# A fifth tile of at most 64 tokens computed in 16 products instead of 24, in a retention and mixture-of-experts kernel

## The chip, the cores and the metric

The kernel runs on one core of a Trainium2 chip. The metric is the device time of one execution in microseconds, the median of several runs. The core has TensorE (PE; PEld is its weight load), VectorE (DVE), ScalarE (ACT), GpSimd (POOL), and SyncE (SP), which issues DMAs; POOL issues the indirect ones (gathers and scatters by row numbers). The engines run beside each other, each through its own instructions in program order, and wait for each other by semaphores.

## What is computed

```python
attn = ((scale * q @ k.T) * Dmat) @ v           # 8 batches, 8 heads, 576 positions, 64 wide; Dmat: causal decay
x = attn.transpose(0, 2, 1, 3).reshape(4608, 512)
logits = normed(x) @ normed(expert_emb).T / tau   # 8 experts
expert_idx = argmax(logits, 1); gate_w = softmax(logits)[expert_idx]
for e in range(8):
    mask = expert_idx == e
    out[mask] = gate_w[mask, None] * (relu(x[mask] @ w1[e]) @ w2[e])   # 512 -> 1024 -> 512
```

All data are float32.

## The kernel before

**Stages.** The first 170 us compute the attention and the routing. Then the experts follow one after another, each in two stages. In the first (mm1, from expert 1 on a list of 28 block products of six matmuls each, in the order `ORDER`) PE computes the hidden layer; in the second (mm2) it multiplies the hidden layer by `w2`. Every float32 operand is kept as a high part and a low part, and a product is the sum of three matmuls: high by high, high by low, low by high.

**Tiles.** An expert has 640 slots for tokens (`CAP`), five tiles of 128. `mm2(e, i)` does tile i: 8 blocks of the hidden layer times three forms, 24 matmuls of 128x512 (L1303) into one PSUM bank, with `hs` (the hidden layer's high and low parts) as weights. ACT then scales the bank by the tokens' gates into `ys[i]` (L1315), and `put_rows` (L1277) scatters its rows to `out` by the row numbers in `sid`; slots without a token have a number out of bounds and are dropped. Gates are gathered by the row numbers in `gid` (L376).

**Counts known only at run time.** `count_left` writes for each expert how many tokens it has beyond 512; PE reads the counts into registers (`rest`). In mm1 each product takes 320 columns if there are over 96 such tokens, 304 if over 64, else 288 (L1234, L1237). In mm2 of experts 1 to 6 the fifth tile is skipped if there are none (L1300).

**Order.** The order on each engine is the order of the code. Two plans put the preparation for the next expert between PE's matmuls: `mm2_plan(e)` has an entry for every third of a tile (0 to 14), `mm1_plan(e)` one for each product (1 to 28). In the fifth tile, which stands under a condition, the tasks come behind all its matmuls. The tasks that matter here: `xturn(n, i)`, a 16-bit copy on ACT (L404) and a transposing DMA on SP's queue (L405), which turns the gathered tokens of the next expert; `xjoin`, `xsums`, `xhigh`, `xlow`, which make the operands of mm1 from them (ACT L411 and L446, DVE L422 to L429 and L450); `w1sum`, `w1hi`, `w1lo`, `w2hi`, `w2lo`, the same for weights (L1145, L1119, L1122; `w1sum(e, 3)` is on POOL).

**Buffers.** `ys` has five tiles. In mm1 they are reused: `follow` (L1249) copies a PSUM bank of block 2 into `ys[4]` behind the 17th product, (6, 2), and the 20th product, (7, 2), adds to the same bank, so that PE may start it only when that copy is done. `w0s` has 8192 columns, of which the weights of mm1 take two times 3584 from expert 1 on.

Of the kernel before, what the change touches and what calls it, by code (L numbers as in the profile page):

```python
# [24 lines left out]
DM = H * D  # L25
NE = 8
FF = 1024
NF = FF // P
NT = N // P
CT = 5  # L30
CAP = CT * P
# [7 lines left out]
HB = P // 2  # L39
HC = CAP // 2  # L40
NPR = NF // 2
# [54 lines left out]
def retention_moe(ctx: ExitStack, tc: tile.TileContext, qk, kn, v0s, vs, w1, w2, head, cst, out):  # L96
# [260 lines left out]

    BEG = group_tiles(B - 3)[0] * P

    def gather(e, i, rows=N):  # L360
        a = e * CT + i
        t = xg[e, i] = raws[(2, 3, 6)[i]] if (e, rows) == (0, BEG) else raws[(i + 1) % 7]
        nc.gpsimd.indirect_dma_start(  # L363
            out=t[:, XO : XO + DM],
            out_offset=None,
            in_=xd[:rows, :],
            in_offset=bass.IndirectOffsetOnAxis(ap=gid[:, a : a + 1], axis=0),
        )

    def gather_gates(e, a0=0, a1=CT):  # L370
        if a0 == 0:
            gts[e] = mg.tile([P, CT], F32, name="gt")
        g = gts[e]
        for i in range(a0, a1):
            a = e * CT + i
            nc.gpsimd.indirect_dma_start(  # L376
                out=g[:, i : i + 1],
                out_offset=None,
                in_=gd[:, :],
                in_offset=bass.IndirectOffsetOnAxis(ap=gid[:, a : a + 1], axis=0),  # L380
            )

    def xsplit(i, u):
# [98 lines left out]
        nc.vector.tensor_copy(sid2, f)  # L482

    left = keep.tile([P, NE], I32, name="left")
    rest = []

    def count_left():

        ps = psm.tile([P, 512], F32, name="m")
        nc.tensor.matmul(ps[:, :NE], ones, run, start=True, stop=True)  # L490
        nc.vector.tensor_scalar(
            out=left, in0=ps[:, :NE], scalar1=-float(CAP - P), scalar2=0.0, op0=ALU.add, op1=ALU.max
        )
        done(ps)

# [582 lines left out]
    with ExitStack() as moe:  # L1078
        mw = moe.enter_context(tc.tile_pool(name="mw", bufs=1))
        hs = mw.tile([P, 2, NF, CAP], F32R, name="hs")  # L1080
        xsb = late["xsb"] = mw.tile([P, 10 * CAP], F32R, name="xsb")
        late["xs1"] = xsb[:, : 2 * NP * C1].rearrange("p (s r n) -> p s r n", s=2, r=NP)
        wsa = mw.tile([P, 28 * P], F32R, name="wsa")
# [189 lines left out]

        puts = []

        def put_rows(rows_of_y, k, rows):
            put = nc.gpsimd.indirect_dma_start(  # L1277
                out=out.rearrange("t (k n) -> (t k) n", k=k),
                out_offset=bass.IndirectOffsetOnAxis(ap=rows, axis=0),
                in_=rows_of_y,  # L1280
                in_offset=None,
                bounds_check=N * k - 1,
                oob_is_err=False,
            )
            for other in puts:
                tc.declare_no_dep(put.ins, other.ins, reason="a scatter writes other rows or other columns")
            puts.append(put)

        last_rows = []

        def mm2(e, i, tasks):
            w = w2s.rearrange("p s (f n) -> p s f n", f=NF)
            a = e * CT + i
            y = ys[i]

            step = DM // 2 if a == NA - 1 else DM
            for n in range(0, DM, step):
                ps = psm.tile([P, 512], F32, name="m")
                last = i == CT - 1 and 0 < e < NE - 1
                with tc.If(rest[e] > 0) if last else nullcontext():  # L1300
                    for j, f in enumerate(SECOND):
                        for k, (hsp, ws) in enumerate(((0, 0), (0, 1), (1, 0))):
                            nc.tensor.matmul(  # L1303
                                ps[:, :step],
                                hs[:, hsp, f, i * P : (i + 1) * P],
                                w[:, ws, f, n : n + step],
                                start=(j == 0 and k == 0),
                                stop=(j == NF - 1 and k == 2),
                            )
                            if not last and step == DM and (3 * j + k) % 8 == 7 and 3 * j + k < 23:  # L1310
                                tasks((3 * j + k) // 8)
                if last:
                    tasks(0)
                    tasks(1)
                nc.scalar.activation(y[:, n : n + step], ps[:, :step], AF.Copy, scale=gts[e][:, i : i + 1])  # L1315
                done(ps)
                k = DM // step
                rows = sid[:, a : a + 1] if k == 1 else sid2[:, n // step : n // step + 1]
                part = (y[:, n : n + step], k, rows)
                if a < NA - 2:  # L1320
                    put_rows(*part)
                else:
                    last_rows.append(part)
            tasks(2)
# [5 lines left out]
        def mm2_plan(e):  # L1330
# [64 lines left out]
        for f, ps in zip(PAIRS, first):  # L1395
# [13 lines left out]
            14: [(count_left,), (xturn, 1, 3)],  # L1409
        }  # L1410
        for g in range(NPR, 2 * NF):
            f, q = PAIRS[g % NF], g // NF
# [3 lines left out]
        for e in range(NE):  # L1416
            if e:
                plan = mm1_plan(e)
                for k, (n, i) in enumerate(ORDER, 1):
                    product(e, n, i)  # L1420
                    follow(n, i)
                    if k < len(ORDER):
                        run_tasks(plan, k)
                highs.pop()()
                w2hi(e, 3)
                lows.pop()()
                w2lo(e, 3)
                held.pop()()
                run_tasks(plan, len(ORDER))
# [203 lines left out]
```

## Time and profile before

| | |
|---|---|
| Median of 3 runs | 554.09 us (553.58 to 556.0) |
| Profiled execution | 554.6 us, of which 552.8 us is the span from the first to the last instruction |
| PE busy | 544.5 us, 98% of the span |
| DVE, ACT, POOL busy | 417.2, 375.8, 240.2 us |
| Granted TensorE clock | 1.00 over the whole span |

An mm1 stage lasts 22.6 to 25.1 us, an mm2 stage of five tiles 27.2 us.
A row of a timeline merges like instructions of one engine that follow each other without a gap: its time runs from the first start to the last end, and "xN" is their number. Matmuls overlap, so that the time from one to the next is not the duration of one. What stands in brackets is the engine's idle time before the row and who ended it.

### The profile page before, as it was taken

The page shows a single profiled execution, that of the slowest core. Times are in us where ns is not written, and L with a number is a line of the kernel's source. Part 1 is how long each engine was busy: PE and PEld are TensorE (multiplying, and loading weights), DVE is VectorE, ACT ScalarE, POOL GpSimd, SP SyncE. Part 2 cuts the span into 40 slices and gives each one's busy share as a digit, 9 for nine tenths or more (in the row PEclk, how much of TensorE's full clock was granted, in tenths as well). Part 3 has the DMA queues.
Part 4 walks back from the last instruction along what each step waited for, and adds up shares of the span by engine and source line. Part 5 has one row for each costly group of instructions (what it writes and reads, how often), then busy time and mean ns, then how long its engine had stood idle before and what let it go on. Part 6 is the DMA issues. An engine that isn't in the chain of part 4 may idle for free. (4 is left out here: it accounts for less than half of the span.)

```text
span 552.8 us, 13528 instructions
## 1 busy us (share of the span) xinstructions
PE 544.5 (98%) x5067; PEld 491.3 (89%) x5067; DVE 417.2 (75%) x939; ACT 375.8 (68%) x700; POOL 240.2 (43%) x233
## 2 busy tenths in 40 slices
PE   8999999999999999999999999999999999999996
PEld 8898988898898899889988988998898899889986
DVE  4856778789875967986896789589978948976810
ACT  1256454457767959967895898589879858957511
POOL 6674435543463661265056207603730750343022
PEclk9999999999999999999999999999999999999999
DMA  9999999968459555847765765557567558641211
GB/s 316 390 392 377 376 319 357 377 254 287 149 195 195 169 184 135 170 145 171 156 179 169 148 154 172 171 158 156 177 172 154 171 173 149 159 133 54 77 39 50
DMA packets 81109, 109.57 MB, mean 198 GB/s; under 512 B 42327, under 2 KB 43771, under 8 KB 81024
## 3 DMA queue, kind: packets, MB, share of 16 engines
q1 hardware_dynamic: 71920, 86.24, 54.1%
q0 software_dynamic: 7696, 19.95, 10.8%
q10 hardware_dynamic: 1408, 2.17, 1.2%
q8 instruction: 62, 1.02, 0.8%
q14 instruction: 23, 0.19, 0.1%
HBM read 80.27 MB, written 19.94 MB: 181 GB/s over the span
## 5 line engine op out<-in xcount | busy, mean ns | idle before, releaser
L1303 PE MATMUL m<-w2s,hs 128*128 128x512 f32 x600 | 138.1, 389 | 0.0
L1303 PEld LDWEIGHTS m<-w2s,hs 128*128 128x128 f32 x600 | 112.4, 188 | 23.2
L1277 POOL DMA_INDIRECT out<-y,sid x41 | 50.3, 1227 | 178.9 <-DVE raw L422 122.7
L1303 PE MATMUL a<-w2s,hs 128*128 128x512 f32 (+1 forms) x360 | 78.8, 375 | 0.0
L1303 PEld LDWEIGHTS a<-w2s,hs 128*128 128x128 f32 x360 | 64.2, 188 | 11.9
L363 POOL DMA_INDIRECT raw<-xd,gid x40 | 44.0, 1101 | 29.4 <-ACT xsb L446 11.8
L376 POOL DMA_INDIRECT gt<-gd,gid x40 | 43.9, 1098 | 19.1 <-issue 12.0
L1187 DVE SCALAR_TENSOR_TENSOR hs<-y,hs 128x320 fp32r<-128x320 f32 x84 | 43.8, 528 | 7.6 <-ACT hs L1194 5.6
L411 ACT COPY raw<-raw 128x1024 uint16<-128x1024 uint16 x35 | 47.9, 1367 | 0.8 <-DMA raw<-raw 0.8
L1194 ACT ACTIVATE hs<-y 128x320 fp32r<-128x320 f32 x84 | 39.4, 476 | 12.6 <-DVE y L1245 11.8
L705 POOL TENSOR_TENSOR kt<-kt,cs 128x512 f32<-128x512 f32 x28 | 28.3, 1042 | 44.9 <-DMA kt<-kn 44.9
L1245 DVE TENSOR_TENSOR y<-a,y 128x320 f32<-128x320 f32 x53 | 25.4, 485 | 29.6 <-ACT y L1249 29.2
L1122 DVE TENSOR_TENSOR w2s<-raw,w2s 128x1024 fp32r<-128x1024 f32 x32 | 39.1, 1221 | 8.4 <-ACT w2s L1119 8.3
L1225 PE MATMUL m<-xsb,w0s 128*128 128x288 f32 (+2 forms) x270 | 43.6, 300 | 0.2
L1225 PE MATMUL a<-xsb,w0s 128*128 128x288 f32 (+2 forms) x270 | 43.2, 300 | 0.0
L1315 ACT ACTIVATE y<-m,gt 128x512 f32<-128x512 f32 x26 | 18.0, 691 | 34.3 <-PE m L1303 34.3
L1225 PEld LDWEIGHTS m<-xsb,w0s 128*128 128x128 f32 x270 | 38.8, 188 | 0.6 <-ACT y L1249 0.6
L1225 PEld LDWEIGHTS a<-xsb,w0s 128*128 128x128 f32 x270 | 38.9, 188 | 0.1
L404 ACT COPY raw<-raw 128x1024 uint16<-128x1024 uint16 x35 | 36.7, 1048 | 0.0
L1119 ACT CAST w2s<-raw 128x1024 fp32r<-128x1024 f32 x32 | 33.4, 1043 | 2.9 <-DMA raw<-w 2.9
L724 POOL TENSOR_TENSOR qkt<-qkt,gsb 128x384 f32<-128x384 f32 x32 | 31.3, 1005 | 5.6 <-issue 3.4
L450 DVE TENSOR_TENSOR xsb<-raw,xsb 128x128 fp32r<-128x128 f32 x70 | 30.5, 483 | 0.0
(259 smaller groups left out, 1177.9 us busy)
## 6 DMA issues: line engine op xcount, KB each, us to landing
raw<-w SPq DMA_DIRECT2D x64, 512.0 KB, 4.0
qkt<-qk SPq DMA_DIRECT2D x28, 576.0 KB, 7.4
xd<-y SPq DMA_DIRECT2D x36, 256.0 KB, 9.4
vt<-vs SPq DMA_DIRECT2D x7, 1152.0 KB, 13.0
kt<-kn SPq DMA_DIRECT2D x7, 1024.0 KB, 10.5
qkt<-qk ACTq DMA_DIRECT2D x4, 288.0 KB, 5.5
qkt<-qk SPq DMA_DIRECT2D x4, 288.0 KB, 5.5
out<-y,sid POOLq DMA_INDIRECT x41, 3.4
```

The source lines that it names most:

```text
L363: nc.gpsimd.indirect_dma_start(out=t[:, XO : XO + DM], out_offset=None, in_=xd[:rows, :], in_offset=bass.IndirectOffsetOnAxis(ap=gid[:, a ...
L376: nc.gpsimd.indirect_dma_start(out=g[:, i : i + 1], out_offset=None, in_=gd[:, :], in_offset=bass.IndirectOffsetOnAxis(ap=gid[:, a : a + 1 ...
L404: nc.scalar.copy(far.rearrange("p (h n) -> p h n", h=2), near.rearrange("p (n h) -> p h n", h=2))
L411: nc.scalar.copy(far.bitcast(U16).rearrange("p (n h) -> p h n", h=2), near.rearrange("p (h n) -> p h n", h=2))
L724: nc.gpsimd.tensor_tensor(out=q, in0=q, in1=gsb[:, p, :], op=ALU.mult)
L1119: nc.scalar.copy(hi, u)
L1122: nc.vector.tensor_tensor(out=lo, in0=u, in1=hi.bitcast(F32), op=ALU.subtract)
L1187: nc.vector.scalar_tensor_tensor(out=lo, in0=part(src), scalar=0.0, in1=hi.bitcast(F32), op0=ALU.max, op1=ALU.subtract)
L1194: nc.scalar.activation(hi, part(src), AF.Relu)
L1225: nc.tensor.matmul(ps[:, :n_cols], w[:, ws, ka, d * P : (d + 1) * P], xop(kx, xsp)[:, d, :n_cols], start=(n in (1, 2, 5) and d == 0 and k ...
L1277: put = nc.gpsimd.indirect_dma_start(out=out.rearrange("t (k n) -> (t k) n", k=k), out_offset=bass.IndirectOffsetOnAxis(ap=rows, axis=0), ...
L1303: nc.tensor.matmul(ps[:, :step], hs[:, hsp, f, i * P : (i + 1) * P], w[:, ws, f, n : n + step], start=(j == 0 and k == 0), stop=(j == NF - ...
```

## The change

1. The fifth tile of experts 1 to 6 (`fitted`) gets a third form. With over 64 tokens in it, it runs the 24 matmuls as before; with none it is skipped; with 1 to 64 it runs 16. For this `both_parts` puts, with four copies on DVE (entry 9 of `mm2_plan`), the first 32 of each 64 columns of the high part and of the low part side by side in two free pieces of `w0s` (`ht`). 128 weight columns then hold 64 tokens twice, and the 16 matmuls are `ht` by high `w2` and `ht` by low `w2`. The copies are made for all six experts, whatever their counts.
2. The low rows of such a tile come out in other partitions of `ys[4]` than the high rows. `low_rows` makes row numbers for the gates (`gidx`) and for the low rows (`sidx`): 11 operations on DVE behind `count_left`, which gets one more itself. The first scatter writes the high rows; `add_low` adds the low rows to `out` with a second, adding scatter from `ys[4]`, issued by POOL behind the 10th product of the next mm1, once the first has landed. It is issued for all six experts; where the tile has no low rows, all its row numbers are out of bounds.
3. `xturn(n + 1, 0)`, the copy on ACT and its transposing DMA, moves from entry 8 of the mm1 stage to entry 12 of the mm2 stage ahead of it, between the fifth tile's matmuls and its scaling on ACT.

```diff
+    def fitted(e, i):
+        return i == CT - 1 and 0 < e < NE - 1
...
+            ids = gidx[:, e : e + 1] if fitted(e, i) else gid[:, a : a + 1]
...
+    def low_rows():
+        q = P // 4
+        g, r = tab[:, 0, :NE], tab[:, 1, :NE]
+        nc.vector.memset(r, BIG)
+        nc.vector.tensor_copy(g, fifth(gid))
+        for k in (0, 2):
+            to, of = slice((k + 1) * q, (k + 2) * q), slice(k * q, (k + 1) * q)
+            nc.vector.tensor_copy(g[to], fifth(gid)[of])
+            nc.vector.tensor_copy(r[to], fifth(sid)[of])
...
+        nc.vector.tensor_scalar(
+            out=few, in0=ps[:, :NE], scalar1=float(CAP - P + HB), scalar2=None, op0=ALU.is_le
+        )
...
+        ht = [w0s[:, o : o + NPR * P].rearrange("p (f c) -> p f c", f=NPR) for o in (28 * P, 4096 + 28 * P)]
...
+                compute_op=ALU.add if first else ALU.bypass,
...
+        def both_parts():
+            for k in range(2):
+                for o, v in enumerate(ht):
+                    t = hs[:, k, NPR * o : NPR * (o + 1), (CT - 1) * P :].rearrange("p f (h c) -> p f h c", h=2)
+                    v = v.rearrange("p f (h s c) -> p f h s c", h=2, s=2)
+                    nc.vector.tensor_copy(v[:, :, :, k, :], t[:, :, :, : HB // 2])
+        def add_low(e):
+            put_rows(ys[CT - 1], 1, sidx[:, e : e + 1], firsts[e])
...
+                if fitted(e, i):
+                    with tc.If(rest[e] > HB) as many:
+                        passes(three)
+                    with many.Else():
+                        with tc.If(rest[e] > 0):
+                            passes(((ht, 0), (ht, 1)))
...
+            if fitted(e, CT - 1):
+                plan[9].insert(1, (both_parts,))
...
+            if n + 1 < NE:
+                plan[12].append((xturn, n + 1, 0))
...
-                plan[8] = [(xturn, n, 0)]
...
+                    if k == 10 and fitted(e - 1, CT - 1):
+                        add_low(e - 1)
```

**Fifth tile of expert 2, on PE**, before; `m_71` and `m_69` are the banks of tiles 2 and 3, `m_68` that of the fifth:

```order
L1303 MATMUL m_69<-w2s,hs 128x512 x24
L1300 COMPARE_AND_BRANCH
L1303 MATMUL m_68<-w2s,hs 128x512 x24
L1300 UNCONDITIONAL_BRANCH
L1300 UNCONDITIONAL_BRANCH [waits PE_49]
L1234 COMPARE_AND_BRANCH
```

and now:

```order
L1349 MATMUL m_69<-w2s,hs 128x512 x24
L1366 COMPARE_AND_BRANCH
L1349 MATMUL m_68<-w2s,hs 128x512 x24
L1366 UNCONDITIONAL_BRANCH
L1369 COMPARE_AND_BRANCH
L1349 MATMUL m_68<-w2s,w0s 128x512 [waits DVE_49]
L1349 MATMUL m_68<-w2s,w0s 128x512
L1349 MATMUL m_68<-w2s,w0s 128x512 [waits DVE_49]
L1349 MATMUL m_68<-w2s,w0s 128x512 x13
L1369 UNCONDITIONAL_BRANCH
L1369 UNCONDITIONAL_BRANCH [waits PE_49]
```

The 16 new matmuls read `w0s`; their first and third wait for DVE, where the old fifth tile waits for nothing.

**The same place on DVE**, before; the `xsb` rows are the last `xlow`, the row behind them is `w1lo(n, 1)`:

```order
L450 TENSOR_TENSOR xsb<-raw_81,xsb 128x4x2x64
L450 TENSOR_TENSOR xsb<-raw_82,xsb 128x2x64
L450 TENSOR_TENSOR xsb<-raw_82,xsb 128x4x2x64
L1122 TENSOR_TENSOR wsa<-wsum,wsa 128x1024
L1145 TENSOR_TENSOR wsum<-raw_83 128x256 x2
```

and now:

```order
L454 TENSOR_TENSOR xsb<-raw_81,xsb 128x4x2x64
L454 TENSOR_TENSOR xsb<-raw_82,xsb 128x2x64
L454 TENSOR_TENSOR xsb<-raw_82,xsb 128x4x2x64
L1331 COPY w0s<-hs 128x8x32 x4
L1152 TENSOR_TENSOR wsa<-wsum,wsa 128x1024
```

The four copies stand behind `xlow` and ahead of `w1lo`.

**The 16th and 17th product of the next mm1, on ACT**, before; `raw_79` is `xturn(n, 1)`, `y_88` is `ys[4]`:

```order
L1119 CAST wsa<-wsum 128x1024 [waits Pool_49]
L1234 UNCONDITIONAL_BRANCH x2
L1194 ACTIVATE hs<-y_85 128x5x64 [waits DVE_49]
L1194 ACTIVATE hs<-m_68 128x5x64 [waits PE_49]
L404 COPY raw_79<-raw_79 128x1024 [waits DMASW0_49]
L1249 COPY y_88<-m_69 128x320 [waits DMASW2_49,PE_49]
```

and now:

```order
L1149 CAST wsa<-wsum 128x1024 [waits Pool_49]
L1264 UNCONDITIONAL_BRANCH x2
L1224 ACTIVATE hs<-y_85 128x5x64 [waits DVE_49]
L1224 ACTIVATE hs<-m_68 128x5x64 [waits PE_49]
L408 COPY raw_79<-raw_79 128x1024 [waits DMASW2_49]
L1279 COPY y_88<-m_69 128x320 [waits DMASW5_49,DMASW4_49,PE_49]
```

The copy into `ys[4]` waits for two scatters out of `ys[4]` where it waited for one. On POOL the adding scatter stands behind the four operations of `w1sum(e, 3)`.

## Rows read from the trace of the kernel before

**Rows 1.** The page, first part: busy time, share of the span, instructions.
```profile
PE 544.5 (98%) x5067; PEld 491.3 (89%) x5067; DVE 417.2 (75%) x939; ACT 375.8 (68%) x700; POOL 240.2 (43%) x233
```

**Rows 2.** Waits of PE's weight loads from 165 us: total, times, longest.
```profile
PEld m L1225 <- ACT y L1249: 1.3, 4, 0.4
```

**Rows 3.** Timeline of PE, experts 2 and 3: start, length, line, tiles, shape, count.
```profile
249.58 1.76 PE L1225 MATMUL a<-xsa,w0s 128*128 128x288 f32 x12
...
272.22 11.07 PE L1303 MATMUL a<-w2s,hs 128*128 128x512 f32 x48
283.13 16.48 PE L1303 MATMUL m<-w2s,hs 128*128 128x512 f32 x72
299.45 1.76 PE L1225 MATMUL a<-xsa,w0s 128*128 128x288 f32 x12
```

**Rows 4.** Timeline of PE, first products of mm1 of experts 1, 5 and 6.
```profile
199.02 1.86 PE L1225 MATMUL a<-xsa,wsa 128*128 128x304 f32 x12
...
394.18 2.02 PE L1225 MATMUL a<-xsa,w0s 128*128 128x320 f32 x12 [0.32 <-PEq L1300]
...
446.52 1.70 PE L1225 MATMUL a<-xsa,w0s 128*128 128x304 f32 x11
```

**Rows 5.** Timeline of DVE, and one row of PEld, around expert 2's fifth tile.
```profile
292.01 1.69 DVE L450 TENSOR_TENSOR xsb<-raw,xsb 128x128 fp32r<-128x128 f32 x4
293.62 1.21 DVE L1122 TENSOR_TENSOR wsa<-wsum,wsa 128x1024 fp32r<-128x1024 f32 x1
...
299.23 1.75 PEld L1225 LDWEIGHTS a<-xsa,w0s 128*128 128x128 f32 x12
...
301.30 0.49 DVE L1245 TENSOR_TENSOR y<-a,y 128x320 f32<-128x320 f32 x1 [3.95 <-ACT y L1249]
```

**Rows 6.** Groups of DVE by line and shape: count, busy us, mean ns.
```profile
L847 DVE COPY xT<-m 128x448 f32<-128x448 f32 x2 | 1.2, 615 | 0.0
L846 DVE COPY xC<-m 128x64 f32<-128x64 f32 x2 | 0.4, 214 | 0.0
L348 DVE CAST gid<-t 128x37 int32<-128x37 f32 x1 | 0.2, 183 | 0.0
L217 DVE TENSOR_SCALAR ss_all<-ss_all 128x36 f32<-128x36 f32 x1 | 0.2, 172 | 0.0
```

**Rows 7.** Timeline of ACT and PEld in the mm1 stage that begins at 299.45.
```profile
299.65 0.69 ACT L1315 ACTIVATE y<-m,gt 128x512 f32<-128x512 f32 x1 [4.03 <-PE m L1303]
...
306.40 1.05 ACT L404 COPY raw<-raw 128x1024 uint16<-128x1024 uint16 x1
...
314.29 0.43 ACT L1249 COPY y<-m 128x320 f32<-128x320 f32 x1
...
314.77 0.82 PEld L1225 LDWEIGHTS m<-xsb,w0s 128*128 128x128 f32 x6 [0.30 <-ACT y L1249]
```

**Rows 8.** Timeline of POOL, around the fifth tile and in the same mm1 stage.
```profile
294.02 1.70 POOL L1277 DMA_INDIRECT out<-y,sid  x1 [0.30 <-issue]
...
308.84 0.88 POOL L1145 TENSOR_TENSOR wsum<-raw,wsum 128x256 f32<-128x256 f32 x1
```

**Rows 9.** All 41 scatters to `out`: from POOL's start to landing.
```profile
DMA to landing us min/median/max: 2.2/3.4/6.1
```

**Rows 10.** Timelines of DVE and POOL: short DVE operations while POOL works.
```profile
115.36 4.05 POOL L705 TENSOR_TENSOR kt<-kt,cs 128x512 f32<-128x512 f32 x4 [7.61 <-DMA kt<-kn]
115.53 0.90 DVE L348 CAST gid<-t 128x3 int32<-128x3 f32 x1
...
527.26 1.00 POOL L1277 DMA_INDIRECT out<-y,sid  x1 [19.53 <-ACT y L1315]
...
527.59 0.17 DVE L482 CAST sid<-f 128x2 int32<-128x2 f32 x1
```

**Rows 11.** Timeline of DVE around `count_left`.
```profile
173.66 0.16 DVE L491 TENSOR_SCALAR left<-a 128x8 int32<-128x8 f32 x1
...
176.72 0.43 DVE L422 TENSOR_TENSOR raw<-raw 128x256 f32<-128x256 f32 x1 [1.76 <-ACT raw L411]
```

More of the change, by code (lines that the diff above doesn't have):

```diff
@@ L379, in gather_gates @@
                 in_=gd[:, :],
-                in_offset=bass.IndirectOffsetOnAxis(ap=gid[:, a : a + 1], axis=0),
+                in_offset=bass.IndirectOffsetOnAxis(ap=ids, axis=0),
             )
@@ L484, in retention_moe, with fifth @@
     left = keep.tile([P, NE], I32, name="left")
+    few = tab[:, 0, NE : 2 * NE]
+    gidx = keep.tile([P, NE], I32, name="gidx")
+    sidx = keep.tile([P, NE], I32, name="sidx")
     rest = []
+    def fifth(t):
+        return t.rearrange("p (e i) -> p e i", i=CT)[:, :, CT - 1]
+    def low_rows():
[7 more added lines that the diff above has]
+            nc.vector.tensor_copy(r[to], fifth(sid)[of])
+        nc.vector.tensor_tensor(out=g, in0=g, in1=fifth(gid), op=ALU.subtract)
+        nc.vector.tensor_tensor(out=g, in0=g, in1=few, op=ALU.mult)
+        nc.vector.tensor_tensor(out=gidx, in0=g, in1=fifth(gid), op=ALU.add)
+        nc.vector.scalar_tensor_tensor(out=r, in0=r, scalar=-BIG, in1=few, op0=ALU.add, op1=ALU.mult)
+        nc.vector.tensor_scalar(out=sidx, in0=r, scalar1=BIG, scalar2=None, op0=ALU.add)
     def count_left():
@@ L1274, in retention_moe, with put_rows @@
         puts = []
-        def put_rows(rows_of_y, k, rows):
+        firsts = {}
+        def put_rows(rows_of_y, k, rows, first=None):
             put = nc.gpsimd.indirect_dma_start(
@@ L1283, in put_rows @@
                 oob_is_err=False,
+                compute_op=ALU.add if first else ALU.bypass,
             )
             for other in puts:
-                tc.declare_no_dep(put.ins, other.ins, reason="a scatter writes other rows or other columns")
+                if other is not first:
+                    tc.declare_no_dep(put.ins, other.ins, reason="a scatter writes other rows or other columns")
             puts.append(put)
+            return put
         last_rows = []
+        def both_parts():
[6 more added lines that the diff above has]
+            put_rows(ys[CT - 1], 1, sidx[:, e : e + 1], firsts[e])
         def mm2(e, i, tasks):
@@ L1298, in mm2, with passes, between @@
                 ps = psm.tile([P, 512], F32, name="m")
-                last = i == CT - 1 and 0 < e < NE - 1
-                with tc.If(rest[e] > 0) if last else nullcontext():
+                def passes(forms, inner=lambda m: None):
+                    m = 0
                     for j, f in enumerate(SECOND):
-                        for k, (hsp, ws) in enumerate(((0, 0), (0, 1), (1, 0))):
+                        for rows, ws in forms:
                             nc.tensor.matmul(
                                 ps[:, :step],
-                                hs[:, hsp, f, i * P : (i + 1) * P],
+                                rows[f // NPR][:, f % NPR] if rows is ht else rows[:, f],
                                 w[:, ws, f, n : n + step],
-                                start=(j == 0 and k == 0),
-                                stop=(j == NF - 1 and k == 2),
-                            )
-                            if not last and step == DM and (3 * j + k) % 8 == 7 and 3 * j + k < 23:
-                                tasks((3 * j + k) // 8)
-                if last:
+                                start=(m == 0),
+                                stop=(m == NF * len(forms) - 1),
+                            )
+                            m += 1
+                            inner(m)
+                def between(m):
+                    if step == DM and m in (8, 16):
+                        tasks(m // 8 - 1)
+                hi, lo = (hs[:, k, :, i * P : (i + 1) * P] for k in range(2))
+                three = ((hi, 0), (hi, 1), (lo, 0))
+                if fitted(e, i):
[4 more added lines that the diff above has]
+                            passes(((ht, 0), (ht, 1)))
                     tasks(0)
                     tasks(1)
+                else:
+                    passes(three, between)
                 nc.scalar.activation(y[:, n : n + step], ps[:, :step], AF.Copy, scale=gts[e][:, i : i + 1])
@@ L1320, in mm2 @@
                 if a < NA - 2:
-                    put_rows(*part)
+                    firsts[e] = put_rows(*part)
                 else:
@@ L1408, in retention_moe @@
             13: [(xturn, 1, 2)],
-            14: [(count_left,), (xturn, 1, 3)],
+            14: [(count_left,), (low_rows,), (xturn, 1, 3)],
         }
```

## Prediction

> **What bounds the kernel now.** I read the page first, then the waits of PE, then single stages. PE is busy 98% of the span [rows 1], so a matmul less is time less, and whatever makes PE wait is time more. Behind the first 170 us its weight loads wait for another engine only four times, 1.3 us in all, each time for ACT's copy at L1249 [rows 2]. One of them is in [rows 7]: the weight load of 314.77 waited 0.30 us and began 0.05 us after the copy that runs from 314.29 to 314.72. DVE and ACT are 75% and 68% busy: they bind only where one operation of theirs is late for PE.
>
> A matmul's duration isn't what it costs. In [rows 3] 72 matmuls of 128x512 begin at 283.13, and the next stage begins at 299.45: 16.32 / 72 = 0.227 us each, 5.44 us per tile.
>
> **Which experts take the new form.** The columns of mm1 tell it: 288 stand for at most 64 tokens in the fifth tile. Expert 2 (mm1 from 249.58) and expert 3 (from 299.45) have 288 [rows 3]; expert 1 has 304, 5 has 320, 6 has 304 [rows 4]. Expert 4 skips its tile: ahead of 394.18 PE waited 0.32 us for its own branch of L1300 [rows 4]. So two experts run 16 matmuls, and four run what they ran.
>
> **Term 1, the matmuls.** 2 experts x 8 matmuls x 0.227 = **-3.6 us**. Neither ACT nor DVE takes it back at the start of the next mm1: there ACT had waited 4.03 us for PE [rows 7] and DVE 3.95 us for ACT [rows 5].
>
> **Term 2, the four copies, which PE must wait for.** The order puts them behind the last `xlow`, and the first of the 16 matmuls waits for the third copy. In expert 2 `xlow` ends at 293.70, and the next operation starts at 293.62, 0.08 ahead of that end [rows 5]; there the copies would begin. PE would load the fifth tile's first weights at 293.79: 48 of the 72 matmuls from 283.13 on bring it to 294.01, and a weight load is 0.22 ahead of its matmul (299.23 and 299.45, [rows 3, 5]). So there is 0.17 us of cover, and the third copy isn't done by then.
>
> A copy has 256 columns a partition. No row shows such a copy within SBUF. From PSUM, 64 columns took 214 ns and 448 took 615 [rows 6]: 1.04 ns a column, so 0.41 us for 256, the upper end. The lower end is 0.17 us, a cast of two columns [rows 10]. I take 0.29, half of the columns' time on a base of 0.16, since 36 columns within SBUF took 172 ns where 37 took 183 [rows 6]: 11 ns for one column more is no full-rate step, and an even count may go at half the price. Each copy starts 0.08 to 0.09 before the last one ends. Third copy done: 293.62 + 2 x 0.20 + 0.29 = 294.31, PE goes on at 294.36, 0.57 late. At 0.41: 293.62 + 2 x 0.33 + 0.41 = 294.69, 0.95 late. At 0.17: 0.23 late. The fourth copy, needed two matmuls later, is no later in any case. Two experts: **+1.1 us** (0.5 to 1.9).
>
> The Trainium skill ("VectorE: DVE Perf Modes", The perf-mode tier table) says that a float32 copy within SBUF runs at twice the rate of a `tensor_tensor`; by it the term would be 1.1, by the copies from PSUM 1.9, and no row here shows the rate of such a copy outright.
>
> In the experts that don't wait, the copies hold up DVE by some 0.9 us; `w1lo` and `w1sum` behind them are needed well into the next mm1, and DVE's 3.95 us idle [rows 5] takes it up. With less cover, 0.9 us for each of six.
>
> **Term 3, the 16-bit copy.** ACT's L404 of 1.05 us [rows 7] leaves the busy mm1 stage, where ACT goes from 306.40 to 314.29 almost without a pause, and comes into the 4.03 us in which ACT waits for the fifth tile. There it is free, also with the tile 1.8 us shorter: 4.03 - 1.8 + 0.6 - 1.05 leaves 1.8. Its tokens were gathered ten entries earlier; its transposing DMA goes ahead of a weight load on SP's queue, which waits for a buffer anyway. In mm1 the copy into `ys[4]` can then come earlier than 314.29 by up to about 0.3 (its product and `xturn(n, 1)` still stand before it), which is just what PE lost at 314.77. Bounds: 0 and the whole 1.3 us of [rows 2]. I take half: **-0.6 us**.
>
> **Term 4, the adding scatter.** It costs POOL six times 1.0 to 1.7 us [rows 8, 10], where POOL would else idle until the next stage's first scatter. What it can cost PE is its landing: the copy into `ys[4]` may not overwrite what the scatter reads, and the 20th product may not start before that copy. POOL ends `w1sum` at 309.72 [rows 8]; 0.30 later, its usual gap, the scatter starts, at 310.02. PE wants to go on at 314.77 - 0.30 = 314.47; with 0.43 for the copy and 0.05 behind it, the scatter must have landed by 313.99. That is **3.97 us** after its start. At 4.27 PE loses the 0.30 that it lost before; from there on every 0.1 us of landing is 0.1 us of PE in each of up to six stages. The scatters of before landed after 2.2 to 6.1 us, median 3.4 [rows 9], and here one transposing DMA fewer is in flight. By the median nothing is lost: **0**, with up to 6 x (6.1 - 4.27) = 11 at the other end.
>
> **Small terms.** `low_rows` and the added comparison are 12 operations of about 0.16, partly overlapping, some 1.2 to 1.9 us; between `count_left` at 173.66 and 176.72 DVE has three microseconds with little in them, 1.76 of them idle in one piece [rows 11], and the operands made there are due some 25 us later (199.02, [rows 4]): 0. The second comparison on PE: mm1 passes a nested pair in every product, and 12 matmuls of two products still follow each other (1.76 us, [rows 3]), so 0; the skip of expert 4, with its 0.32 us [rows 4], is the worst that I can find, 6 x 0.3 = 1.9 at most. The gate gathers are as many as before.
>
> **Sum.** -3.6 + 1.1 - 0.6 + 0 = -3.1 us. On the profiled execution, 554.6 (span 552.8 and 1.8 around it), that gives 551.5; that execution lies 0.5 over the median of 554.09, on which the same sum gives **551.0**. A measurement of this kernel can tell about 0.5% from no change, 2.8 us; the forecast is barely beyond that.
>
> **Rival 1: DVE's copies come later than I think (no change).** Either they take the full 0.41, and the sum is -3.6 + 1.9 - 0.6 = -2.3, 551.8; or POOL holds them up. A cast of three columns took 0.90 us [rows 10] while POOL's multiplications ran (115.36 to 119.41), against 0.17 to 0.18 elsewhere, so POOL can stop a copy of DVE until its own operation ends. At the fifth tile POOL runs a scatter from 294.02 to 295.72 [rows 8]. If that held back the third copy, it would end at 295.72 + 0.29 = 296.0, PE 2.3 late: 2 x 2.3 - 3.6 - 0.6 = +0.4, 554.5. Against it: a cast of two columns under such a scatter, at 527.59, took 0.17 [rows 10].
> The Trainium skill ("SBUF — State Buffer", Who interferes with whom) has the rule for it: DVE copies in a two-port mode and GpSimd share a port pair, and whoever starts first holds it for its whole instruction. By that rule this rival would come true; the cast at 527.59 speaks against it for scatters, with one row.
>
> **Rival 2: the adding scatter lands late (slower).** It must read `out` before it writes, which no scatter of before did, and the longest of those took 6.1. If it lands x us after 4.27 in six stages, the sum is -3.6 + 1.1 + 6x; it is slower by over 2.8 us from x = 0.88, a landing of 5.2 us. At 5.7 it is -2.5 + 8.6 = +6.1: 560. If only the two experts with real rows are late (at 5.7), it is -2.5 - 0.3 + 2.9: 554, no change. For it: the longest plain landing is already past that point [rows 9]. Against it: the median, 1.8 us short of it, and the transposing DMA that leaves this stage.
>
> **Rival 3: the change doesn't do what it says.** If the counts were other than the columns tell, or branches ate the gain at 0.3 each, the sum is about -3.1 + 1.9 = -1.2 or above: 553 to 554.
>
> **How the numbers follow.** Forecast 0.50, with 550.2 to 551.9 for its own range (term 2 from 0.5 to 1.3, term 3 from 0 to 1.3); some 0.06 of it is less than 0.5%. Rival 1 0.20, rival 2 0.22, of which 0.14 slower and 0.08 no change, rival 3 0.08. Faster 0.45 (0.44 of the forecast, a little of rival 1), same 0.41, slower 0.14. The range holds the forecast, rival 1, the mild half of rival 2 and rival 3: 550.0 to 555.5. Left out are the late landings, 0.14, and some 0.05 below.
>
> **What the profile after would show.** Term 1: two tiles with 16 matmuls from `w0s`, in experts 2 and 3, none elsewhere. Term 2: PE idle ahead of these 16, put down to the copies, 0.6 us each; over 1.5 us, with a copy as long as POOL's scatter, is rival 1. Term 3: no wait of PE for L1249's copy at the 20th product. Term 4: landings of the adding scatters around 3.5; waits of ACT for a scatter at the copy into `ys[4]`, and PE behind it, are rival 2. What would make me wrong most is a landing above 5 us.

## The result, and the profile after

The changed kernel takes **560.5 us** (558.5 to 560.9, 6 runs) where the kernel before took 554.5 in the same comparison: ratio **1.0102** [1.0085, 1.0118], 1% slower. 551.0 was forecast, with a range up to 555.5. The profiled execution took 559.64 us (span 557.6).

The page, first part (as [rows 1]):

```profile
PE 542.4 (97%) x5051; PEld 490.1 (88%) x5051; DVE 419.0 (75%) x975; ACT 377.8 (68%) x700; POOL 256.8 (46%) x239
```

PE runs 16 matmuls fewer than in [rows 1], two times 8. It has less work and takes longer. What it waits for, from 165 us on (as [rows 2]: total, times, longest):

```profile
PEld m L1255 <- ACT y L1279: 7.9, 4, 2.7
PEld a L1255 <- issue: 1.4, 2, 0.7
PEld m L1349 <- DVE w0s L1331: 0.9, 2, 0.6
```

The first row was 1.3 us in [rows 2] (L1225 and L1249 are now L1255 and L1279). It is the 20th product behind ACT's copy into `ys[4]`. What ACT waited for before these copies (waits of ACT, the same stretch):

```profile
ACT y L1279 <- DMA out<-y,sidx: 8.1, 4, 3.1
```

`sidx` holds the row numbers of the adding scatter. The chain is in one place in the mm1 stage of expert 4, which begins at 345.76 (timelines of POOL, ACT and PEld, as [rows 7, 8]; landing of the two scatters out of `ys[4]` that start at 349.44 and 357.42, from the views of their row numbers in that stretch):

```profile
349.44 1.29 POOL L1309 DMA_INDIRECT out<-y,sid  x1 [0.30 <-issue]
...
355.43 0.75 POOL L1175 TENSOR_TENSOR wsum<-raw,wsum 128x256 f32<-128x256 f32 x1
357.42 2.20 POOL L1309 DMA_INDIRECT out<-y,sidx  x1 [1.23 <-DVE y L1275]
...
359.74 1.04 ACT L408 COPY raw<-raw 128x1024 uint16<-128x1024 uint16 x1
363.52 0.43 ACT L1279 COPY y<-m 128x320 f32<-128x320 f32 x1 [2.75 <-DMA out<-y,sidx]
...
364.00 0.83 PEld L1255 LDWEIGHTS m<-xsb,w0s 128*128 128x128 f32 x6 [2.47 <-ACT y L1279]
```

```profile
DMA to landing us min/median/max: 7.7/7.7/7.7
DMA to landing us min/median/max: 6.0/6.0/6.0
```

The first scatter, from 349.44, lands 7.7 us later at 357.1. Only then may POOL start the second, at 357.42, though its own work was done at 356.2. (The row names an operation of DVE as the releaser; that it is the landing shows in the 0.28 us between the two: in mm1 of expert 5, where the row names the first scatter, the second starts 0.27 us behind that landing.) The second one lands 6.0 us later at 363.4; ACT copies at 363.52; PE goes on at 364.00, 2.47 us late.

The stages, from a stage's first matmul to that of the next (from PE's timelines; as [rows 3, 4]):

| Stage | before | after | difference |
|---|---|---|---|
| mm2 of experts 2 and 3 | 27.23, 27.22 | 25.95, 25.64 | -1.28, -1.58 |
| mm1 of expert 2 | 22.64 | 22.36 | -0.28 |
| mm1 of expert 3 | 22.65 | 23.81 | +1.16 |
| mm1 of expert 4 | 22.59 | 27.02 | +4.43 |
| mm1 of expert 5 | 25.12 | 27.45 | +2.33 |
| mm1 of expert 6 | 23.33 | 24.68 | +1.35 |

From the start of expert 0's mm2 to PE's last matmul this makes 382.7 us against 376.5: -2.9 in mm2, +9.0 in these mm1 stages, less than 0.1 in the others. That stretch is compared below, since what lies ahead of it varied by 4 us between the profiles of changed kernels, which are all alike there (in the first profile after it was 1.6 us shorter than before).

### The profile page after: what moved, and what is told of

Read it like the earlier page. It is cut to its first block, busy times and chain, and to the rows that moved or that the text cites. A ratio compares the mean times of both kernels' runs of the same rounds, so it can differ in the third digit from the quotient of the medians.

```text
span 557.6 us, 13552 instructions
## 1 busy us (share of the span) xinstructions
PE 542.4 (97%) x5051; PEld 490.1 (88%) x5051; DVE 419.0 (75%) x975; ACT 377.8 (68%) x700; POOL 256.8 (46%) x239
## 5 line engine op out<-in xcount | busy, mean ns | idle before, releaser
L1349 PE MATMUL m<-w2s,hs 128*128 128x512 f32 x552 | 127.2, 389 | 0.0
L1349 PEld LDWEIGHTS m<-w2s,hs 128*128 128x128 f32 x552 | 103.4, 188 | 21.3
L1255 PE MATMUL m<-xsb,w0s 128*128 128x288 f32 (+2 forms) x270 | 44.7, 304 | 4.4 <-ACT y L1279 4.4
L380 POOL DMA_INDIRECT gt<-gd,gid x34 | 39.7, 1169 | 17.1 <-issue 9.8
L1217 DVE SCALAR_TENSOR_TENSOR hs<-y,hs 128x320 fp32r<-128x320 f32 x84 | 42.6, 513 | 4.8 <-ACT hs L1224 2.8
L1255 PEld LDWEIGHTS m<-xsb,w0s 128*128 128x128 f32 x270 | 39.8, 191 | 5.2 <-ACT y L1279 5.2
L1255 PE MATMUL a<-xsb,w0s 128*128 128x288 f32 (+2 forms) x270 | 43.5, 301 | 0.4 <-issue 0.4
L1255 PEld LDWEIGHTS a<-xsb,w0s 128*128 128x128 f32 x270 | 39.2, 188 | 0.7 <-issue 0.7
```

What stands on the lines that cost most here:

```text
L380: nc.gpsimd.indirect_dma_start(out=g[:, i : i + 1], out_offset=None, in_=gd[:, :], in_offset=bass.IndirectOffsetOnAxis(ap=ids, axis=0),)
L1217: nc.vector.scalar_tensor_tensor(out=lo, in0=part(src), scalar=0.0, in1=hi.bitcast(F32), op0=ALU.max, op1=ALU.subtract)
L1255: nc.tensor.matmul(ps[:, :n_cols], w[:, ws, ka, d * P : (d + 1) * P], xop(kx, xsp)[:, d, :n_cols], start=(n in (1, 2, 5) and d == 0 and k ...
L1349: nc.tensor.matmul(ps[:, :step], rows[f // NPR][:, f % NPR] if rows is ht else rows[:, f], w[:, ws, f, n : n + step], start=(m == 0), stop ...
```

## Experiments

There are seventeen runs in five groups (e1 to e4, e5 to e8, e9 to e12, e13 to e15, e16 and e17), each group beside its own runs of the kernel before, which took 557.5, 554.3, 554.6, 557.4 and 557.7 us in them: a ratio holds for its group. The same kernel differed by up to 0.4% between groups (e1 and e9, e14 and e17), so that smaller differences across groups show nothing. In profiles of the first group and of e13, PE's completions also reached ACT up to 3 us late near the 8th product of mm1, in kernels with different edits alike, so I lean on the other profiles. PE's stretch is that from the start of expert 0's mm2 to the last matmul (376.5 before, 382.7 after), in one execution each.

| Run | Edit | Ratio [95%] | PE's stretch |
|---|---|---|---|
| e1 | after, buffer of its own for the copy | 0.9994 [0.9974, 1.0014] | 381.5 |
| e2 | after, no adding scatter | 1.0000 [0.9976, 1.0025] | 378.9 |
| e3 | after, second scatter plain | 1.0025 [1.0002, 1.0048] | 379.4 |
| e4 | after, 16-bit copy back | 1.0077 [1.0045, 1.0109] | 379.7 |
| e5 | before, again | (one run) | 377.9 |
| e6 | before, 16-bit copy moved | 1.0029 [1.0008, 1.0050] | 377.8 |
| e7 | e1, four copies and `xturn(n, 1)` moved | 1.0086 [1.0060, 1.0113] | 379.5 |
| e8 | after, again | 1.0100 [1.0070, 1.0131] | 382.4 |
| e9 | e1, again | 0.9952 [0.9928, 0.9976] | 373.7 |
| e10 | shorter tile alone | 0.9954 [0.9934, 0.9974] | 373.9 |
| e11 | e1, 16-bit copy back | 0.9977 [0.9957, 0.9997] | 375.3 |
| e12 | e1, gathers later | 0.9942 [0.9922, 0.9962] | 374.1 |
| e13 | e3, again | 1.0017 [0.9988, 1.0045] | 378.9 |
| e14 | after, gathers later | 0.9993 [0.9968, 1.0018] | 375.4 |
| e15 | e12, four copies first at entry 9 | 0.9888 [0.9859, 0.9918] | 373.4 |
| e16 | e15, again | 0.9889 [0.9867, 0.9912] | 373.6 |
| e17 | e14, again | 0.9958 [0.9936, 0.9980] | 375.7 |

**e1 and e9: does the wait for `ys[4]` make the loss?**

```diff
-            ya, yb, yc = ys[min(i, 1)], ys[2 + i % 3], ys[0]
+            ya, yb, yc = ys[min(i, 1)], wsum_t if i == 2 else ys[2 + i % 3], ys[0]
```

> The changed kernel, but the copy of the product (6,2) goes into wsum_t, which is idle then, and no longer into ys[4], from which the adding scatter reads. Theory (the copy into ys[4] waits for the adding scatter's landing, and PE behind it): the four stalls of PE at the 20th product (1.2 to 2.7 us) are gone, with them the stretch at clock 0.5, every mm1 stage is back at 22.6 to 23.4 (25.1 for expert 5), time about 551.5 (554.5 less the 2.9 us of two shorter tiles). Rival (the second scatter's work on POOL, on the queue and on the DMA engines costs the time, or the moved transpose does): the stages stay long by several us, time 557 to 560.

> The same kernel as the first run (the copy of (6,2) into wsum_t), timed again, since in the first call the kernel before took 557.5 us and in the second 554.3. Theory (the second scatter's landing was the whole loss): ratio 0.995 and no wait of PE over 0.5 us in mm1. Rival (the plain scatters land late too, since the transpose now runs beside them, and the copies into ys[2] and ys[3] wait for these): waits of ACT for plain scatters of 2 to 4 us in mm1 of experts 3, 4 and 5, ratio 0.998 to 1.001.

e1 came out at 0.9994, 557.5 us, which is the time of its rival, but in the group where the kernel before takes 557.5 as well and whose profiles have the late completions. e9, the same kernel, is at 0.9952, 2.7 us below before. Its adding scatters land no sooner (groups of `sidx`, after and e9: POOL's duration, landing):

```profile
L1309 POOL DMA_INDIRECT out<-y,sidx x6: 1604/1650/2397, 258.6 to 512.5; - x6
...
DMA to landing us min/median/max: 3.7/4.7/6.0
```

```profile
L1309 POOL DMA_INDIRECT out<-y,sidx x6: 1605/1620/2394, 258.3 to 503.3; - x6
...
DMA to landing us min/median/max: 3.6/4.9/5.4
```

But nothing waits for them (waits of PE's weight loads in e9):

```profile
PEld m L1255 <- ACT wsum L1279: 1.0, 2, 0.8
PEld a L1255 <- issue: 1.0, 2, 0.7
PEld m L1349 <- DVE w0s L1331: 0.8, 2, 0.4
```

So the loss is the sharing of `ys[4]`, not the work of the second scatter: the two kernels differ in the buffer alone. What is left of the wait there, 1.0 us, is no landing: in expert 3 the copy starts at 311.46, right behind ACT's work ahead of it (to 311.24) and DVE's last read of `wsum_t` (to 311.37).

**e2 and e10: without the adding scatter.** e10 also puts the 16-bit copy back at entry 8 of mm1.

```diff
-                    if k == 10 and fitted(e - 1, CT - 1):
-                        add_low(e - 1)
```

> The changed kernel without the adding scatters (leaves out the low rows' part of the sum for experts 2 and 3). Theory: nothing writes out of ys[4] behind the first scatter any more, so it gives the same as with a buffer of its own, 551.5 within 1 us. Rival (second scatter's own work costs): faster than with a buffer of its own by the several us that it costs there. Rival (the moved transpose or the four copies cost it): stays at 557 to 560 here as well.

> The changed kernel without the adding scatters and with the 16-bit copy back at entry 8 of mm1 (leaves out the low rows' part of the sum for experts 2 and 3): the kernel before with the shorter fifth tile, its four copies and the branch alone. By terms 1 and 2 as measured in the trace (two mm2 stages 1.3 and 1.6 us shorter): 2.9 us less, ratio 0.9948. Rival: with the mm1 stages earlier by this, their copies come closer to the plain scatters' landings and wait for them: under half of it arrives, ratio 0.998 to 1.000.

e2 equals e1 within their intervals (1.0000, 0.9994), though both miss the 551.5 that was expected. e10 is at 0.9954, 2.6 us less: terms 1 and 2 arrive in full. What the scatters cost beyond the buffer is small and not settled: e11 (below) has them, a buffer of its own and the 16-bit copy in the same place as e10, and is 1.3 us slower (0.9977), with intervals that overlap.

**e3 and e13: is it the adding?**

```diff
-                compute_op=ALU.add if first else ALU.bypass,
+                compute_op=ALU.bypass,
```

> The changed kernel with the second scatter as a plain write, still behind the first one's landing (leaves out the sum: the low rows overwrite). Theory that adding itself makes the landing late: landings fall from 3.75 to 6.0 to the plain scatters' median of 3.4, the stalls shrink to under 0.5 us, time 552 to 554. Rival: any second scatter there comes too late, since it starts 10.6 to 13.5 us into mm1 and has to wait for the first one: landings and stalls stay, time 558 to 560.5.

> The changed kernel with the second scatter as a plain write behind the first one's landing, again (leaves out the sum: the low rows overwrite). If adding is what lands late (3.6 to 6.0 us, and 1.6 to 2.4 us on POOL against 1.0): the plain one lands within 3 to 3.5 us, the waits at the 20th product are under 0.7 us, ratio 0.996 to 0.999. If any second scatter comes too late there: as the changed kernel, 1.007 to 1.010.

1.0025 and 1.0017, between e1 and after, both in groups with the late completions, so the price in time is rough. (e3's 559.3 us is the time of its rival, but beside 557.5.) The profile of e13 (group of `sidx`):

```profile
L1309 POOL DMA_INDIRECT out<-y,sidx x6: 1003/1009/1012, 260.6 to 509.4; - x6
...
  ACT y L1279: 1.1, 2
```

The plain scatter takes POOL 1.0 us in place of 1.6 to 2.4, and ACT waits for it 1.1 us, twice, in place of 8.1, four times. Its starts are as late as in after (10.8 to 13.2 us into mm1). That most of the loss is the adding is not shown by this: in mm1 of experts 2, 4 and 5 ACT reaches its copy 1.2 to 2.2 us later than in after, which hides a wait. In mm1 of experts 3 and 6 ACT comes when it does in after, and its copy starts 3.9 and 4.7 us behind the plain scatter's start, against 4.8 and 4.6 behind the adding one's. Landings of the plain ones are not in that profile.

**e4, e6 and e11: the 16-bit copy.** e4 and e11 put it back (in after and in e1), e6 moves it in the kernel before:

```diff
+            if n + 1 < NE:
+                plan[12].append((xturn, n + 1, 0))
...
-                plan[8] = [(xturn, n, 0)]
```

> The changed kernel with the 16-bit copy back at entry 8 of mm1. If the moved transpose is what delays the landings of the first scatter and the gathers at the border of mm2 and mm1 (and so the start of the adding scatters, 11.3 to 13.5 us into mm1 against 10.6): starts return to 10.6, landings to about 4, time 554 to 557. If it has no part in it: 560.5 to 561.5 (ACT's 1.04 us copy is back ahead of the copy into ys[4]).

> The kernel before with one edit: the 16-bit copy and its transpose moved from entry 8 of mm1 to the end of mm2. By term 3 the 0.3-us waits for the copy into ys[4] go: ratio 0.9988 (0.6 us less), at best 0.9977. Rival: the transpose next to the first scatter and the gathers makes these land later (4.3 to 6.9 us in place of 3.7 to 5.7) and what hangs on them gives the gain back: 1.000 to 1.004.

> The copy of (6,2) into wsum_t and the 16-bit copy back at entry 8 of mm1. If the moved transpose is what makes plain scatters land late: no waits of ACT for plain scatters over 2.5 us, the 0.3-us waits at the 20th product are back, ratio 0.995 to 0.997, below the run without the move back by 1 us or more. If it is not: as that run, within 0.5 us.

In e6 the 0.3-us waits are gone: mm1 of experts 2, 3 and 4 lasts 22.27, 22.26 and 22.22 us against 22.65, 22.65 and 22.61 in e5, together -1.2. But mm1 of expert 5 grows from 26.45 to 27.47. What ACT waits for there (waits of ACT in e5, then in e6):

```profile
ACT y L1249 <- DMA out<-y,sid: 3.3, 2, 2.3
```

```profile
ACT y L1249 <- DMA out<-y,sid: 4.7, 2, 4.2
```

A plain scatter is late there in both, and later in e6. That the transpose beside it is why isn't shown: the kernel before took 25.12 and 26.45 us for this stage in two executions. Gain and loss cancel in PE's stretch (377.9 and 377.8), and the timed runs are even 0.3% slower, as the rival had it. With a buffer of its own the move does pay: putting it back costs 1.4 us (e11 0.9977, e9 0.9952; the intervals overlap, PE's stretches are 375.3 and 373.7). e11's expectation, a gain of 1 us or no change, was not met. With the transpose back, the first scatters of experts 2, 3 and 4 land 10.6, 11.3 and 14.4 us into the next mm1 (e11), against 10.4, 11.4 and 13.3 in after, and the adding scatters start at 10.5 to 14.6 us (e4, 1.0077: 10.8 to 13.9): the moved transpose is not what delays them.

**e5 and e8: both kernels again**, on the chip of the second group.

> The kernel before, unchanged, as a profile from the chip of these runs. On the chip of the first four runs PE also waits at the 8th product of mm1 for a copy by ACT (0.4 to 1.3 us, in experts 1, 2, 4 and 5), which the first profile of the kernel before does not show. If that wait belongs to the chip and not to the change, it stands here as well (at least 3 such waits, 2 to 4 us in sum) wherever this chip shows it in the changed kernel; if the change brought it, none stands here.

> The changed kernel, unchanged, timed and profiled on the same chip as the others, so that all stand beside one kernel before. As in the first comparison: ratio 1.0102 (1.0085 to 1.0118), with PE's four waits at the 20th product of 1.2 to 2.7 us for the copy into ys[4].

e8 repeats the result (1.0100) and the waits for the adding scatter (8.6 us, four times). e5 has no wait at the 8th product, and one of 0.95 us in mm1 of expert 5 for a plain scatter, which the first profile did not show. e8 has none at the 8th product either, and the record names the same chip for the first and the second group: what makes completions late in one and not in the other stays open.

**e7: a repair that made it worse.** On top of e1:

```diff
-                plan[9].insert(1, (both_parts,))
+                plan[7].append((both_parts,))
...
-                plan[16] = [(xturn, n, 1)]
+                plan[20] = [(xturn, n, 1)]
```

> The changed kernel with three repairs: the copy of (6,2) into wsum_t, the four copies at entry 7 in place of 9 of mm2, and the 16-bit copy of the second tile (xturn(n, 1)) at entry 20 in place of 16 of mm1, behind the copies that PE waits for. If what was left in the run with a buffer of its own is ACT standing behind its 1.04-us copy at entry 16 (PE waits 0.4 to 0.9 us at the 20th product) and the 0.4-us waits for the four copies: 3 to 4 us below that run, ratio to the kernel before 0.993 to 0.995. Rival: something else keeps it there (the place in mm1 at the 8th product), ratio 0.998 to 1.000.

1.0086 in place of 0.994. Waits of ACT in e7:

```profile
ACT y L1279 <- DMA out<-y,sid: 9.0, 4, 4.1
```

Now plain scatters are late, those out of `ys[2]` and `ys[3]`. Timelines of POOL at the end of expert 2's mm2, in e9 (mm1 begins at 296.09), e7 (298.09) and e12 (299.55):

```profile
290.39 1.23 POOL L366 DMA_INDIRECT raw<-xd,gid  x1 [2.02 <-ACT xsb L450]
291.93 2.50 POOL L1309 DMA_INDIRECT out<-y,sid  x1 [0.30 <-issue]
```

```profile
292.64 3.97 POOL L366 DMA_INDIRECT raw<-xd,gid  x1 [2.02 <-ACT xsb L450]
296.92 1.01 POOL L1309 DMA_INDIRECT out<-y,sid  x1 [0.30 <-ACT raw L408]
```

```profile
292.12 1.07 POOL L1309 DMA_INDIRECT out<-y,sid  x1 [0.31 <-ACT xsa L450]
...
294.80 1.08 POOL L366 DMA_INDIRECT raw<-xd,gid  x1 [0.30 <-DVE xsb L454]
```

In e9 the third tile's scatter stands behind a gather that waits 2.02 us for its buffer, and starts 4.2 us ahead of mm1. In e7 that gather takes 3.97 us and the scatter starts 1.2 ahead; all scatters behind it come 1.5 to 3 us later. In e12 the gather stands behind it, and it starts 7.4 ahead. Which of e7's two moves stretched the gather was not tried by itself.

**e12, e14 and e17: the gathers behind the scatters.**

```diff
-                    plan[(2, 4, 7, 8, 11)[i]].append((gather, n + 1, i))
+                    plan[(2, 5, 8, 8, 11)[i]].append((gather, n + 1, i))
```

> The copy of (6,2) into wsum_t, and the gathers of the second and third tile one place later in mm2 (entries 5 and 8 in place of 4 and 7), so that on POOL the scatter of the third tile no longer stands behind a gather that waits for its buffer. If the place of the plain scatters in POOL's queue sets what ACT waits for: the third tile's scatter starts some 3 us earlier (right behind its tile), the fourth's and fifth's 1 to 3 us earlier, waits for plain scatters under 0.5 us, ratio 0.992 to 0.995. If they land late for another reason (the DMA engines): no better than the run without this, 0.996 to 1.000.

> The changed kernel with the gathers of the second and third tile one place later in mm2, the buffer ys[4] still shared. The adding scatter's start has a floor at 10.6 us into mm1 (behind w1sum on POOL); where it was at 11.3 to 13.5 for the first scatter's landing it comes 0.5 to 2 us earlier: waits at the 20th product 0.5 to 1.5 us in place of 1.2 to 2.7, ratio 1.002 to 1.006. If the start is set by the first scatter's landing whatever the order on POOL, no change: 1.008 to 1.010.

> The changed kernel with the gathers later and the shared buffer, again. By its first profile (starts of the adding scatters 0 to 1.5 us earlier, waits of ACT for them 2.7 us in two places in place of 8.1 in four): about 5 us less than the changed kernel, ratio 0.999 to 1.002 beside a kernel before of 554.5 us. If the order on POOL does not matter: 1.008 to 1.010.

e12 is at 0.9942, with no wait for a plain scatter in mm1; a wait of 1.18 us in mm1 of expert 4, put down to "issue", stays unexplained. e14 and e17 keep the shared buffer: the adding scatters of experts 1 to 3 start 10.55 to 10.57 us into mm1, at their floor, where after has 10.57, 11.27 and 11.66, and expert 4's at 12.0 and 12.1 against 13.5. Expert 5's stays at 12.0. ACT's wait for the adding scatters falls from 8.1 us in four places to 2.4 in two, those of experts 2 and 5 (waits of ACT in e17):

```profile
ACT y L1279 <- DMA out<-y,sidx: 2.4, 2, 1.5
```

PE's stretch falls from 382.7 to 375.4 and 375.7, by 7 of the 9 us that the buffer of its own gives. (e14's profile is of its shortest run, 551.6 us beside a median of 556.6; e17's 553.8 is near its median of 554.5.) So most of the loss goes with earlier starts alone. Landings are not in these two profiles; where ACT waited in e17, its copy began 4.9 and 4.6 us behind the scatter's start, as in after (4.8 and 4.6).

**e15 and e16: the four copies first**, on top of e12:

```diff
-                plan[9].insert(1, (both_parts,))
+                plan[9].insert(0, (both_parts,))
```

> The copy of (6,2) into wsum_t, the gathers later, and the four copies first at entry 9 of mm2, ahead of the two last low parts (0.97 us of DVE). The two waits of 0.35 to 0.37 us for the third copy go: 0.7 us below the run without this, ratio 0.993; the low parts, and with them the last xsa and xsb tile, come 0.8 us later, which costs nothing as long as the first product that reads them is over 1 us away. Rival: that cover is not there, the gain is given back at the first products of mm1, ratio 0.994 to 0.996.

> The copy of (6,2) into wsum_t, the gathers later, the four copies first at entry 9, again. Beside a kernel before of 554.5 us: ratio 0.993 (550.8 us), the stages as in its first profile. If its first ratio of 0.989 was of the kernel and not of the call: 0.989 again.

PE's two waits for the copies are gone, and PE's stretch is 373.4 and 373.6, 0.5 to 0.7 below e12. At 550.8 and 551.6 us this is, with e12 (551.0), the fastest version and beats both kernels: 0.989 beside a kernel before of 557.4 and 557.7, as e12 is 0.994 beside 554.6. That it is faster than e12 is not shown by the times. The expected 0.993 was for a kernel before of 554.5; the kernel's time agrees, and the kernel before differs between groups.

## Why the prediction was wrong

**Term 1 (-3.6) was right.** Two tiles run 16 matmuls, in experts 2 and 3 (timeline of PE, as [rows 3]):

```profile
281.26 11.04 PE L1349 MATMUL m<-w2s,hs 128*128 128x512 f32 x48
292.49 3.98 PE L1349 MATMUL m<-w2s,w0s 128*128 128x512 f32 x16 [0.18 <-DVE w0s L1331]
296.31 1.75 PE L1255 MATMUL a<-xsa,w0s 128*128 128x288 f32 x12
```

**Term 2 (+1.1) had the right mechanism and was 0.3 too large**: mm2 is 2.86 us shorter, so 0.8 of the 3.6 went to the wait. PE waited 0.60 in expert 2, as forecast (0.57), and 0.29 in expert 3. The four copies (timeline of DVE, and their group: count, busy, mean ns):

```profile
291.74 0.89 DVE L1331 CAST w0s<-hs 128x256 fp32r<-128x256 f32 x4
```

```profile
L1331 DVE CAST w0s<-hs 128x256 fp32r<-128x256 f32 x24 | 5.4, 286 | 0.0
```

286 ns where 0.29 was taken. **Rival 1 didn't happen**: the copies were not held up, though POOL's scatter ran beside them (292.16 to 294.66). It was POOL that was slow: that scatter took 2.50 us, against 1.70 in [rows 8]. The Trainium skill ("SBUF — State Buffer", Who interferes with whom) says that of a DVE copy in a two-port mode and GpSimd, whoever issues first has the shared ports for its whole instruction, and the copies came first here. But in experts 3 and 4 a scatter that started in the same place beside the copies took 1.01 us, so what made this one longer is open.

**Term 3 (-0.6) was right in direction and half of the size**: without landings in the way it is -1.2 (e6, three stages) or -1.4 (e9 against e11), the whole 1.3 of [rows 2]. In after it shows only in mm1 of expert 2 (-0.28), where no landing is in the way. That something gives it back in the kernel before (e6, 0.3% slower) was not in the sum.

**Term 4 (0) is the step that failed**; some 9.0 us was its price (382.7 - 373.7, after against e9, which differs in the buffer alone; it holds the half-clock stretch below), and rival 2 came true. The prediction had the mechanism, the place and the limit in the stage that it read: the second scatter had to land by 10.57 + 3.97 = 14.5 us into mm1. (By PE's waits in after, the limit was some 16.2 us with the 320 columns of expert 5 and 15.2 with the 304 of expert 6.) In after the landings were at 14.3, 15.9, 17.7, 18.9 and 16.5 in mm1 of experts 2 to 6, and PE's waits there 0, 1.45, 2.47, 2.69 and 1.25. Two values were wrong:

- *The landing.* 3.4, the median of plain scatters, was taken for an operation that no row showed. It was 3.7 to 6.0. The median was taken over the wrong rows, too. The trace of before has a landing for 35 of the 41 scatters: the 29 that start outside the mm1 stages landed after 3.2 us in the median, the six that start in one, as the new one does, after 4.2 to 6.1, median 5.4. With 5.4, rival 2's own formula gives 559. "Must read before it writes" stood in rival 2 as an argument and moved no number in the sum; how much later the adding itself makes a landing is open (e13).
- *The start.* 10.57 was read in one stage and taken for all, where it is the floor: the second scatter waits for POOL's `w1sum` of its own stage, and also for the first scatter's landing, a wait that the change itself adds. In the kernel before, the first scatter in mm1 of expert 5, which begins at 394.18 [rows 4], and the last operation of `w1sum` stand here (timeline of POOL, and the scatter's landing):

```profile
402.68 1.12 POOL L1277 DMA_INDIRECT out<-y,sid  x1 [0.30 <-issue]
...
406.03 0.88 POOL L1145 TENSOR_TENSOR wsum<-raw,wsum 128x256 f32<-128x256 f32 x1
```

```profile
DMA to landing us min/median/max: 4.2/4.2/4.2
```

Both ended 12.7 us into mm1, already past the floor. In after the start there was 13.5, 0.27 behind the landing. And term 1 itself moved the rest: where the fifth tile became 1.3 to 1.6 us shorter, mm1 began earlier while POOL's row of gathers and scatters, which ACT and DVE set, did not. In mm1 of expert 3 the first scatter started 6.0 us into the stage, against 3.0 before: 1.3 of this is the shorter tile, the rest POOL's own instructions ahead of it (a scatter of 2.50 us for 1.70, a gather of 1.96 for 0.97). `w1sum` behind it ended at 11.1, and the second scatter started at 11.3. In mm1 of expert 4 `w1sum` ended at 10.4 and the first landing, at 11.4, set the start of 11.7. In mm1 of expert 6 the start was 11.97, with `w1sum` done at 10.7 and the first landing at 9.2; what it waited for is open. e14 and e17 show that the start counts.

The 560 of rival 2 is close to the result by luck: its make-up is not the measured one. Four stages lost, not six, by 1.2 to 4.4 us, from starts as much as from landings. It had 0.14 for slower, for "the median, 1.8 us short of it". With six landings to go, the upper end of the spread was the value to weigh.

In mm1 of expert 4 there is more than the wait. Windows of that stage (length; busy time of PE, PEld, DVE, ACT, POOL; granted clock, DMA share, GB/s):

```profile
363.30:365.50 2.20, 1.50 (x11) 1.50 (x12) 0.74 (x2) 1.98 (x5) 0.00 (x0) 0.99 0.27 57
365.50:368.80 3.30, 3.30 (x16) 3.30 (x15) 2.72 (x5) 2.25 (x5) 0.00 (x0) 0.50 0.30 101
368.80:372.78 3.98, 3.98 (x31) 3.98 (x31) 2.95 (x6) 3.38 (x7) 0.00 (x0) 0.99 0.61 204
```

For 3.3 us PE ran at half clock (1.2 GHz), 16 matmuls where 31 follow in 3.98: some 1.2 us of the 4.43. It came 1.5 us behind the 2.47-us wait; but e8 has waits of 2.75 and 2.69 us and no such stretch, so that the wait caused it is not shown. A further 0.66 us is a wait of PE's weight loads earlier in the stage, put down to "issue", whose cause is open.

## What to carry to other kernels

A new reader of a buffer is priced by the next writer of that buffer: find its time, start from the last event in the new operation's own list of waits, do both in every stage and not in one, take the spread from rows that stand in the same kind of stage, and take its late end when several instances must all be in time. A stage that gets shorter on one engine makes everything that other engines do beside it later for the next stage; look at which of that was just in time. On a queue that runs in order, a transfer that somebody waits for should not stand behind one that waits for a buffer itself.

## What the runs showed that I had not expected

- The adding scatter took POOL 1.60 to 2.40 us, the plain one in its place 1.00 (e13), and made more packets (page, DMA packets of before, of after and of e13): 865 more for six adding scatters, 481 for six plain ones.

```profile
DMA packets 81109, 109.57 MB, mean 198 GB/s; under 512 B 42327, under 2 KB 43771, under 8 KB 81024
```

```profile
DMA packets 81974, 109.79 MB, mean 197 GB/s; under 512 B 43094, under 2 KB 44538, under 8 KB 81888
```

```profile
DMA packets 81590, 109.78 MB, mean 198 GB/s; under 512 B 42757, under 2 KB 44201, under 8 KB 81504
```

- By the counts in [rows 3, 4] four of the six adding scatters (experts 1, 4, 5, 6) have no row to add: their row numbers are all out of range. Those of experts 1, 4 and 5 landed 3.7, 5.3 and 4.5 us after their start in after, where the two with rows took 4.7 and 6.0; in e8 it was 3.6, 5.4 and 4.9 against 5.4 and 4.6. A scatter with nothing to write is not free here.
- The same gather took 1.23 us in e9 and 3.97 in e7, the same scatter 1.00, 1.70 or 2.50, and the place of a scatter on POOL's queue moved PE by several us. What sets these durations was not tried by itself.
- In e2 ACT waited 10.7 us for PE's completions, up to 3.0 at once (waits of ACT), with PE's matmuls on time; after has 1.1 at most. The cause is open.

```profile
ACT y L1279 <- PE m L1255: 10.7, 9, 3.0
```
